# Zero products, row-block results, casts and exponents' arguments placed anew at the start of a retention and feed-forward kernel

## The chip, the cores and the metric

The kernel runs on one core of a Trainium2 chip. A core has TensorE (PE; its weight loads are listed as PEld), VectorE (DVE), ScalarE (ACT), GpSimd (POOL) and SyncE (SP, which here issues the loads). The metric is the device time in microseconds (us), lower is better. Four runs of the kernel before gave 191.04, 191.81, 189.85 and 191.72 us, median 191.38.

## The reference

Four batches, eight heads, 768 positions, head size 64. Each head keeps a 64x64 state that decays by a factor of its own, and the result goes through a multiplicative feed-forward block:

```python
gamma = 1.0 - 2.0 ** (-5.0 - np.arange(H))
for t in range(S):
    state = gamma * state + einsum('bhd,bhe->bhde', k[:, :, t], v[:, :, t])
    y[:, :, t] = scale * einsum('bhd,bhde->bhe', q[:, :, t], state)
x = y.transpose(0, 2, 1, 3).reshape(B * S, H * D)      # 3072 x 512
a = x @ w1                                             # 512 x 1024
b = x @ w2                                             # 512 x 1024
h = a * b @ w3                                         # 1024 x 1024
out = h @ w_out                                        # 1024 x 512
```

## The kernel before

**The whole.** The recurrence is computed by chunks of 128 positions: masked products of queries and keys within a chunk (`scores`, `intra`), plus the effect of the state carried over (`kv`, `state`, `inter`). The decays are folded into scale factors: `VS` on the values, `YS` on the outputs, `GS` on the state. Nothing is multiplied between `w3` and `w_out`, so the kernel first computes their product, `W3O = w3 @ w_out`, in eight row blocks of 128 rows. Then it goes through 12 steps of two batches and one chunk each; a step does attention for one chunk and the feed-forward products of the chunks before. The first two units are special: `Pairs(0)` and `Pairs(1)`, named b0 and b1, are two chunks together of batch 0 and of batch 1.

**Order.** The order is written by hand (`manual_schedule`): each engine executes its instructions as they stand in the program, and each waits for what it reads and for the buffer that it writes.

**The start, in which the change lies.** SP issues all loads in one row (lines 131 to 157): pieces of `w3` and `w_out`, then `q`, `k`, `v` of batch 0, `w1`, the same of batch 1, `w2`, and the later chunks. They land in a ring of 22 stages (`stg`). At most eight loads are under way, since each waits for the one eight places ahead of it.

For row blocks 0 to 5, one block `f` goes in two halves `h`. `cast_w3(f, h)` (line 246) casts half a block to 16 bits: on VectorE for the first halves of blocks 0 to 3, on ScalarE for the others (they show as L239). `w3_half(f, h)` (line 262) transposes it with four TensorE products (L269) and lets VectorE copy the result to `w3t` (L274). `cast_wo(i)` casts two of the eight row groups of `w_out`, half on ScalarE (L243), half on GpSimd (L244). `w3_part(f, i)` (line 293) adds two products of 128x512 (L298) to the accumulator `acc[f]`, a bank of PSUM; with i = 3, the last two, it also lets VectorE copy the bank to `W3O[f]` (L303). Accumulators 0 and 1 lie in banks Y0 and Y1, which the transposes of batch 0's queries and keys take over; 2 to 5 lie in a pool of four banks, from which rows 6 and 7 and then the feed-forward products take theirs.

Row blocks 6 and 7 are done whole: `cast_w3_row` (L255), `w3_transpose` (L280, with a copy to `w3t` on ScalarE, L239), and `W3Block`, whose `mm` adds products (L312) and whose `back` copies the bank to `W3O` on ScalarE (L319).

`busy(m, f)` (line 723) puts m products of zeros, 128x256, into the accumulator of block f before its first real product starts it anew. They compute nothing that is used.

`output_decays()` (line 216) makes `YS`: three products of 128x256 on VectorE (L219, the exponents' arguments `ys_x`), and for each an exponential on ScalarE (L223).

b0 and b1 follow: `q_cast` and `k_cast` (L333), transposes (L371; their copies show as L237 on VectorE), scores (L472) with a mask on VectorE (`am`, L479), `intra` (L493), `kv` (L510), `state` (L521), `inter` (L541), `outputs_back` (L552), and the next state (L526 on VectorE, then L533 on GpSimd). Between their steps stand the first feed-forward products of `w1` and `w2` (`by_rows`, L838), whose four banks include the one of row block 7, and the casts of `w1` (L817) and `w2` (L871, L872, L884). The later steps' products show as L679 and L706.

Of the kernel before, what the change touches and what calls it, by code (L numbers as in the profile page):

```python
# [18 lines left out]
def kernel(  # L19
# [11 lines left out]
    nc = tc.nc  # L31
# [176 lines left out]
    def decays():  # L208
        for h in range(H):
            for s in range(2):  # L210
                nc.gpsimd.memset(LGP[half((h + s) % 2), s, h // 2 : h // 2 + 1], math.log(gam[h]))
        for h in range(H):
            p, r = h // 2, (h % 2) * 64
            nc.gpsimd.memset(GS[r : r + 64, p : p + 1], gam[h] ** C)

    def output_decays():
        for n, (s, swap) in enumerate(((0, 0), (1, 0), (1, 1))):
            x = fsb.tile([128, NP, L], FP, tag="pa", name="ys_x", bufs=8)
            nc.vector.tensor_tensor(  # L219
                x[:, :, :], if_f[:, s, :].unsqueeze(1).broadcast_to((128, NP, L)),  # L220
                LGP[:, swap, :].unsqueeze(2).broadcast_to((128, NP, L)), MULT,
            )
            nc.scalar.activation(YS[:, n, :, :], x[:, :, :], AF.Exp)  # L223
# [7 lines left out]
    W3O = [wpool.tile([128, DM], HP, name=f"w3o_{i}") for i in range(8)]  # L231
# [3 lines left out]
    def cast_to(dst, src, on_dve):  # L235
        if on_dve:
            nc.vector.tensor_copy(dst, src)  # L237
        else:
            nc.scalar.copy(dst, src)  # L239

    def cast_wo(i):
        dst = WO[i][:, :, :].rearrange("p a n -> p (a n)")
        nc.scalar.copy(dst[:, 0:512], wo_st[i][:, 0:512])  # L243
        nc.gpsimd.tensor_copy(dst[:, 512:1024], wo_st[i][:, 512:1024])  # L244

    def cast_w3(f, h):
        W3h[f, h] = att.tile([128, 1024], HP, tag="qT", name="w3h", bufs=5)
        cast_to(W3h[f, h][:, 0:512], w3_st[f][:, h * 512 : h * 512 + 512], h == 0 and f < 4)

    def cast_w3_row(f, *engs):  # L250
        W3h[f] = att.tile([128, 1024], HP, tag="qT", name="w3h", bufs=5)
        n = 1024 // len(engs)
        for i, eng in enumerate(engs):
            cs = slice(i * n, i * n + n)
            (nc.scalar.copy if eng is nc.scalar else eng.tensor_copy)(W3h[f][:, cs], w3_st[f][:, cs])  # L255

    def bank(tag, shape, dtype, name):
        return ps_at.tile(shape, dtype, tag=tag, name=name)
# [3 lines left out]
    def w3_half(f, h):  # L262

        src = W3h.pop((f, h))
        ps = bank(("X0", "X1")[len(units) % 2], [128, 512], HP, "psW3")
        units.append(f)
        for g in range(4):
            c0 = (g // 2) * 256 + g % 2
            nc.tensor.transpose(  # L269
                ps[:, g * 128 : (g + 1) * 128], src[:, c0 : c0 + 255 : 2], ident16[:, :]  # L270
            )
        if h == 0:
            w3t[f] = att.tile([128, 1024], HP, tag="k16" if f < 3 else "v16", name="w3t", bufs=3)
        nc.vector.tensor_copy(w3t[f][:, h * 512 : h * 512 + 512], ps[:, :])  # L274

    def w3_transpose(f, on_dve):
        src, ps = W3h.pop(f), ps_f.tile([128, 1024], HP, tag="psF", name="psW3")
        for g in range(8):
            c0 = (g // 2) * 256 + g % 2
            nc.tensor.transpose(  # L280
                ps[:, g * 128 : (g + 1) * 128], src[:, c0 : c0 + 255 : 2], ident16[:, :]
            )
        w3t[f] = att.tile([128, 1024], HP, tag="k16" if f == 6 else "v16", name="w3t", bufs=3)
        cast_to(w3t[f][:, :], ps[:, :], on_dve)

    acc = {}

    def acc_of(f):
        if f not in acc:
            acc[f] = bank(f"Y{f}", [128, DM], FP, "psW") if f < 2 else ps_f.tile([128, DM], FP, tag="psF", name="psW")  # L290
        return acc[f]

    def w3_part(f, *parts):

        for i in parts:
            for r in range(2):
                g = i * 2 + r
                nc.tensor.matmul(  # L298
                    acc_of(f)[:, :], lhsT=w3t[f][:, g * 128 : (g + 1) * 128], rhs=WO[i][:, r, :],
                    start=(g == 0), stop=(g == 7),  # L300
                )
            if i == 3:
                nc.vector.tensor_copy(W3O[f][:, :], acc[f][:, :])  # L303

    class W3Block:
        def __init__(self, f):
# [8 lines left out]
                )  # L315
            self.g += n

        def back(self):
            nc.scalar.copy(W3O[self.f][:, :], self.ps[:, :])  # L319

    q16s, k16s, v16s, qTs, kTs, AMs, psYs, Ts = {}, {}, {}, {}, {}, {}, {}, {}

    def q_cast(n, *engs):
        if n not in q_in:
            return
        q16s[n] = att.tile([128, 1024], HP, tag="q16", name="q16", bufs=2)
        pairs_cast(q16s[n], q_in.pop(n), *engs)

    def pairs_cast(dst, src, *engs):
        n = H // len(engs)  # L330
        for i, eng in enumerate(engs):
            hs = slice(i * n, i * n + n)
            (nc.scalar.copy if eng is nc.scalar else eng.tensor_copy)(  # L333
                dst[:, :].rearrange("i (t h d) -> i h t d", t=2, d=D)[:, hs, :, :],
                src[:, :].rearrange("i (h t d) -> i h t d", t=2, d=D)[:, hs, :, :],
            )
# [24 lines left out]
    def q_transposes(n, tag, on_dve):  # L361
        qTs[n] = att.tile([128, 2, NP, 128], HP, tag="qT", name="qT", bufs=5)
        pairs_transposes(qTs[n], q16s.pop(n), tag, on_dve)
# [359 lines left out]
    def busy(m, f, n=512):  # L723

        for _ in range(m):
            nc.tensor.matmul(acc_of(f)[:, 0:n], lhsT=Z[:, 0:128], rhs=Z[:, 0:n], start=True, stop=True)
# [2 lines left out]
    busy(12, 0, 256)  # L729
    w3_half(0, 0)  # L730
    cast_wo(0)
    busy(4, 0, 256)
    cast_w3(1, 0)
    w3_part(0, 0)
    w3_half(1, 0)
    busy(1, 1, 256)
    cast_w3(2, 0)
    w3_half(2, 0)
    w3_part(1, 0)
    cast_w3(3, 0)  # L740
    w3_half(3, 0)
    w3_part(2, 0)
    cast_wo(1)
    masks()
    cast_w3(4, 0)
    cast_w3(5, 0)
    cast_w3(0, 1)
    busy(1, 4, 256)
    w3_part(3, 0)
    busy(1, 4, 256)  # L750
    for f in range(4):
        w3_part(f, 1)
    w3_half(4, 0)
    cast_wo(2)
    decays()
    w3_half(5, 0)
# [7 lines left out]
    w3_half(2, 1)  # L764
    w3_part(1, 2)
    cast_wo(3)
    cast_w3(3, 1)
    w3_part(2, 2)
    w3_half(3, 1)
    output_decays()  # L770
    cast_w3(4, 1)
    cast_w3(5, 1)
    for f in range(3):
        w3_part(f, 3)
    q_cast(0, nc.gpsimd)
    w3_part(3, 2, 3)
    q_transposes(0, "Y0", True)
    w3_half(4, 1)
    w3_half(5, 1)
    b0, b1 = Pairs(0), Pairs(1)  # L780
    b0.k_cast(nc.vector)
    w3_part(4, 2, 3)
    w3_part(5, 2)
    b0.k_transposes("Y1", True)
    w3_part(5, 3)
    cast_w3_row(6, nc.scalar, nc.gpsimd)
    am_back = b0.scores(0)
    am_back(0)
# [6 lines left out]
    wb = W3Block(6)  # L795
# [7 lines left out]
    last = ended(b0.intra(1), nc.vector)  # L803
    b0.outputs_back(0)
    wb.mm(2)
    wb.back()
    w3_transpose(7, False)
    b0.inter(last)
    b0.next_state_add()
    b0.outputs_back(1)  # L810
    wb = W3Block(7)
# [7 lines left out]
    cast_w1_halves(0, nc.scalar, nc.gpsimd)  # L819
    cast_w1_halves(1, nc.scalar, nc.gpsimd)  # L820
    wb.mm(6)
    wb.back()
    q_cast(1, nc.scalar, nc.gpsimd)
    b1.k_cast(nc.scalar)
    b1.v_cast(nc.gpsimd, 0)
# [203 lines left out]
```

## Time and profile before

| | |
|---|---|
| median of four runs | 191.38 us |
| the profiled execution | 191.04 us, its span 189.3 us |
| mean granted TensorE clock | 0.989 of full |
| busy: PE, PEld, DVE, ACT, POOL | 175.2, 125.7, 111.6, 71.8, 69.0 us |
| PE busy in 0 to 5, 5 to 10, 20 to 25 us | 3.59, 2.25, 2.91 us |
| PE busy in 50 to 60, 60 to 70 us | 9.90, 10.00 us |
| DVE busy in 20 to 25 us | 4.80 us |
| L303 (results of blocks 0 to 5), DVE | 6 of 679 ns |
| L219 (exponents' arguments), DVE | 3 of 623 ns |
| L223 (exponentials), ACT | 3 of 417 ns |
| L333 (batch 0's keys on DVE; batch 1's on ACT) | 678 ns; 1047 ns |
| L533 (product of 128x256, two inputs), POOL | 2 of 612 ns |

A group's line gives the source line, engine, operation, the tiles out and in, the size and the count. The granted clock is the share of its full clock that TensorE's throttle let through. Idle time of an engine matters only where something on the path to the end waits for that engine. Lengths of instructions that follow each other on an engine overlap a little, so starts lie somewhat closer than lengths.

### The profile page before, as it was taken

The page shows a single profiled execution, that of the slowest core. Times are in us where ns is not written, and L with a number is a line of the kernel's source. Part 1 is how long each engine was busy: PE and PEld are TensorE (multiplying, and loading weights), DVE is VectorE, ACT ScalarE, POOL GpSimd, SP SyncE. Part 2 cuts the span into 40 slices and gives each one's busy share as a digit, 9 for nine tenths or more (in the row PEclk, how much of TensorE's full clock was granted, in tenths as well). Part 3 has the DMA queues.
Part 4 walks back from the last instruction along what each step waited for, and adds up shares of the span by engine and source line. Part 5 has one row for each costly group of instructions (what it writes and reads, how often), then busy time and mean ns, then how long its engine had stood idle before and what let it go on. Part 6 is the DMA issues. An engine that isn't in the chain of part 4 may idle for free.

```text
span 189.3 us, 6242 instructions
## 1 busy us (share of the span) xinstructions
PE 175.2 (93%) x2635; PEld 125.7 (66%) x2635; DVE 111.6 (59%) x214; ACT 71.8 (38%) x158; POOL 69.0 (36%) x125
## 2 busy tenths in 40 slices
PE   7489588968999999999999999999999999999993
PEld 4145354636785769688596785867858688585872
DVE  2424996165165977864847657467495674946330
ACT  3164525712764033243333433424334243332432
POOL 3175252501982294084411836126434260000000
PEclk9999999997999999999999999999999999999999
DMA  5999999999899989979998999989999980110203
GB/s 171 361 401 338 338 372 273 353 382 229 185 274 210 180 276 218 162 201 242 192 217 176 184 240 154 262 175 229 279 172 209 223 167 3 59 55 3 111 0 113
DMA packets 80396, 39.72 MB, mean 210 GB/s; under 512 B 57457, under 2 KB 74097, under 8 KB 80369
## 3 DMA queue, kind: packets, MB, share of 16 engines
q1 hardware_dynamic: 79936, 38.81, 88.7%
q10 hardware_dynamic: 432, 0.52, 0.7%
q8 instruction: 20, 0.33, 0.7%
q14 instruction: 8, 0.06, 0.1%
HBM read 29.36 MB, written 6.29 MB: 188 GB/s over the span
## 4 chain that ended last, share of the span: by engine, by line
PE 72%; DMA 10%; SPq 9%; issue 5%; ACT 1%; POOL 1%; ACTq 0%; POOLq 0%
PE psF L679 39%; PE psO L706 22%; DMA stg<-in_moe_w_dram 10%; SPq L63 9%; PE psY L574 2%; PE psY L642 2%; PE psA L426 2%; PE psF L838 2%; PE psK L594 1%; PE psTk L400 1%; PE psG L679 1%; POOL w L871 1%; ACT w L239 1%; PE psTq L371 0%; ACT osb L710 0%
## 5 line engine op out<-in xcount | busy, mean ns | idle before, releaser
L679 PE MATMUL psF<-xt,w 128*128 128x256 f16 x672 | 76.5, 273 | 0.0
L679 PEld LDWEIGHTS <-w 128*128 128x128 f16 x704 | 68.4, 98 | 11.2 <-issue 0.8
L694 DVE TENSOR_TENSOR ht<-pa,psF 128x256 f16<-128x256 f32 x88 | 36.9, 421 | 37.1 <-PE psF L679 31.4
L706 PE MATMUL psO<-w3o,ht 128*128 128x512 f16 (+2 forms) x200 | 43.9, 371 | 0.0
L688 ACT COPY pa<-psF 128x256 f32<-128x256 f32 x80 | 29.7, 372 | 37.1 <-PE psF L679 37.1
L706 PEld LDWEIGHTS <-ht 128*128 128x128 f16 x200 | 18.5, 98 | 19.4
L710 ACT ACTIVATE osb<-psO 128x512 f32<-128x512 f32 (+2 forms) x25 | 14.5, 580 | 43.5 <-PE psO L706 42.4
L657 DVE TENSOR_TENSOR xt<-psY,YS 64x512 f16<-64x512 f32 (+1 forms) x29 | 21.1, 728 | 4.8 <-PE psY L642 4.4
L353 POOL TENSOR_TENSOR v<-stg,VS 128x512 f16<-128x512 f32 x20 | 20.5, 1043 | 0.8 <-DMA stg<-in_v_dram 0.7
L346 POOL CAST k<-stg 128x512 f16<-128x512 f32 x18 | 10.9, 613 | 21.9 <-DMA stg<-in_k_dram 15.6
L609 POOL TENSOR_TENSOR t<-s,GS 128x512 f16<-128x512 f32 x8 | 8.3, 1040 | 24.5 <-DVE s L608 24.5
L333 POOL CAST q<-stg 128x1024 f16<-128x1024 f32 (+1 forms) x12 | 12.0, 1005 | 12.1 <-DMA stg<-in_q_dram 11.2
L298 PE MATMUL psW<-wo,w3t 128*128 128x512 f16 x48 | 12.5, 380 | 2.7 <-DVE w3t L274 1.7
L433 DVE TENSOR_TENSOR am<-psA,keep 128x512 f16<-128x512 f32 x20 | 12.8, 682 | 0.6 <-PE psA L426 0.6
L838 PE MATMUL psF<-xt,w 128*128 128x256 f16 x64 | 9.8, 297 | 0.2
L274 DVE COPY w3t<-psW 128x512 f16<-128x512 f16 x12 | 4.9, 421 | 7.6 <-PE psW L269 7.6
L298 PEld LDWEIGHTS <-w3t 128*128 128x128 f16 x48 | 4.0, 97 | 6.8 <-DVE w3t L274 3.4
L838 PEld LDWEIGHTS <-w 128*128 128x128 f16 x64 | 6.3, 105 | 2.4 <-ACT w L239 0.4
L616 DVE TENSOR_TENSOR t<-psK,t 128x512 f16<-128x512 f32 x9 | 6.2, 690 | 0.7 <-PE psK L594 0.5
L269 PEld LDWEIGHTS <-w3h 128*128 128x128 f16 x48 | 3.2, 98 | 5.1 <-DVE w3h L237 3.7
L269 PE MATMUL psW<-ident,w3h 128*128 128x128 f16 x48 | 4.5, 220 | 2.1 <-DVE w3h L237 2.0
L458 POOL TENSOR_TENSOR v<-stg,VS 128x512 f16<-128x512 f32 x4 | 4.1, 1042 | 5.1 <-DMA stg<-in_v_dram 2.9
(89 smaller groups left out, 150.4 us busy)
## 6 DMA issues: line engine op xcount, KB each, us to landing
stg<-in_q_dram SPq DMA_DIRECT2D x12, 512.0 KB, 7.1
out_dram<-osb SPq DMA_DIRECT2D x22, 256.0 KB, 3.0
stg<-in_moe_w_dram SPq DMA_DIRECT2D x10, 512.0 KB, 8.6
stg<-in_k_dram SPq DMA_DIRECT2D x20, 256.0 KB, 5.3
stg<-in_v_dram SPq DMA_DIRECT2D x20, 256.0 KB, 6.0
stg<-in_moe_w_dram SPq DMA_DIRECT2D x12, 256.0 KB, 6.9
stg<-in_moe_w_out_dram SPq DMA_DIRECT2D x4, 512.0 KB, 6.9
stg<-in_k_dram SPq DMA_DIRECT2D x2, 512.0 KB, 9.8
```

The costliest lines, as they stand in the source:

```text
L63: nc.sync.dma_start(dst, src)
L298: nc.tensor.matmul(acc_of(f)[:, :], lhsT=w3t[f][:, g * 128 : (g + 1) * 128], rhs=WO[i][:, r, :], start=(g == 0), stop=(g == 7),)
L333: (nc.scalar.copy if eng is nc.scalar else eng.tensor_copy)(dst[:, :].rearrange("i (t h d) -> i h t d", t=2, d=D)[:, hs, :, :], src[:, :]. ...
L353: eng.tensor_tensor(v16[:, e, :].rearrange("j (h d) -> j h d", d=D), v32[:, e, :].rearrange("j (h d) -> j h d", d=D), VS[:, 2, :].unsqueez ...
L433: nc.vector.tensor_tensor(am[:, r, :, :], ps[r][:, :, :], keep[:, :].unsqueeze(1).broadcast_to((128, NP * 2, L)), MULT,)
L657: nc.vector.tensor_tensor(XT[m][to, :, s, :].rearrange("p (a e) (i t) -> p a e t i", e=2, t=2), psYs[m][s][fr, :, :].rearrange("p (a e) (t ...
L679: nc.tensor.matmul(ps[:, :], lhsT=W[d][:, f * 128 : (f + 1) * 128], rhs=self.x(d), start=(d == 0), stop=(d == 3),)
L688: nc.scalar.copy(self.pa[f][:, :], ps[:, :])
L694: nc.vector.tensor_tensor(self.HT[:, f, :], self.pa.pop(f)[:, :], ps[:, :], MULT)
L706: nc.tensor.matmul(psO[:, :], lhsT=self.HT[:, f, e * 128 : (e + 1) * 128], rhs=W3O[f][:, cs], start=(f == 0), stop=(f == 7),)
L710: nc.scalar.activation(osb[:, cs], psO[:, :], AF.Copy, scale=final_scale)
L838: nc.tensor.matmul(ps[f // 2][:, f % 2, :], lhsT=W[d][:, f * 128 : (f + 1) * 128], rhs=f0.x(d), start=(d == 0 and f % 2 == 0), stop=(d == ...
```

## The change

Five things are done to the order of the first 48 us; the amount of real work stays as it is.

1. `output_decays()` makes its three products on GpSimd, and is called one step earlier: ahead of `cast_w3(3, 1)`.
2. The copies of the results of row blocks leave `w3_part` and become calls of their own, `w3_back(f, on_dve)`: blocks 0, 2, 3, 4 on VectorE, 1 and 5 on ScalarE, each at a place of its own.
3. The products of blocks 2 and 3 with the second group of `w_out` move behind the transposes of `(4, 0)`; block 3's last products are split around the transposes of batch 0's queries.
4. Casts: batch 0's keys go from VectorE to ScalarE. With `wb.back(True)`, row block 7's result goes from ScalarE to VectorE, which takes it out of the way of batch 1's queries and keys on ScalarE. Row block 6's result comes behind the copy of the transposes of row 7.
5. Seven more products of zeros: 4 to 6, 1 to 2 at three places, and 2 new ones ahead of `w3_half(3, 0)`.

```diff
@@ output_decays
-            nc.vector.tensor_tensor(
+            nc.gpsimd.tensor_tensor(
                 x[:, :, :], if_f[:, s, :].unsqueeze(1).broadcast_to((128, NP, L)),
...
@@ w3_part
-            if i == 3:
-                nc.vector.tensor_copy(W3O[f][:, :], acc[f][:, :])
+
+    def w3_back(f, on_dve):
+        cast_to(W3O[f][:, :], acc[f][:, :], on_dve)
...
@@ W3Block
-        def back(self):
-            nc.scalar.copy(W3O[self.f][:, :], self.ps[:, :])
+        def back(self, on_dve=False):
+            cast_to(W3O[self.f][:, :], self.ps[:, :], on_dve)
...
     w3_half(0, 0)
     cast_wo(0)
-    busy(4, 0, 256)
+    busy(6, 0, 256)
     cast_w3(1, 0)
     w3_part(0, 0)
     w3_half(1, 0)
-    busy(1, 1, 256)
+    busy(2, 1, 256)
     cast_w3(2, 0)
     w3_half(2, 0)
     w3_part(1, 0)
     cast_w3(3, 0)
+    busy(2, 3, 256)
     w3_half(3, 0)
...
-    busy(1, 4, 256)
+    busy(2, 4, 256)
     w3_part(3, 0)
-    busy(1, 4, 256)
-    for f in range(4):
-        w3_part(f, 1)
+    busy(2, 4, 256)
+    w3_part(0, 1)
+    w3_part(1, 1)
     w3_half(4, 0)
+    w3_part(2, 1)
+    w3_part(3, 1)
...
     cast_wo(3)
+    output_decays()
     cast_w3(3, 1)
     w3_part(2, 2)
     w3_half(3, 1)
-    output_decays()
+    w3_part(0, 3)
+    w3_back(0, True)
+    q_cast(0, nc.gpsimd)
     cast_w3(4, 1)
+    w3_part(1, 3)
+    w3_part(2, 3)
+    w3_part(3, 2)
     cast_w3(5, 1)
-    for f in range(3):
-        w3_part(f, 3)
-    q_cast(0, nc.gpsimd)
-    w3_part(3, 2, 3)
     q_transposes(0, "Y0", True)
     w3_half(4, 1)
+    w3_part(3, 3)
     w3_half(5, 1)
+    w3_back(1, False)
+    w3_back(2, True)
+    w3_back(3, True)
     b0, b1 = Pairs(0), Pairs(1)
-    b0.k_cast(nc.vector)
+    b0.k_cast(nc.scalar)
     w3_part(4, 2, 3)
     w3_part(5, 2)
     b0.k_transposes("Y1", True)
     w3_part(5, 3)
+    w3_back(4, True)
+    w3_back(5, False)
     cast_w3_row(6, nc.scalar, nc.gpsimd)
...
     wb.mm(2)
+    w3_transpose(7, False)
     wb.back()
-    w3_transpose(7, False)
     b0.inter(last)
...
     wb.mm(6)
-    wb.back()
+    wb.back(True)
     q_cast(1, nc.scalar, nc.gpsimd)
     b1.k_cast(nc.scalar)
     b1.v_cast(nc.gpsimd, 0)
```

## The prediction

> **What bounds the kernel now.** I read first the chain of work that ended last, then each engine's timeline up to 50 us, then the granted clock by stretches. Rows of the chain give start, length (us) and work; rows of a timeline start, length, engine, line, operation, tiles, and in brackets the idle time before and what ended it.
>
> ```profile
> PE 72%; DMA 10%; SPq 9%; issue 5%; ACT 1%; POOL 1%; ACTq 0%; POOLq 0%
> ...
> 30.81 6.80 DMA stg<-in_moe_w_dram
> 37.66 0.61 POOL w L817
> 38.27 8.54 issue
> ...
> 47.40 1.05 POOL w L871
> 48.49 1.05 PE psF L838 x8
> ```
>
> From 48.49 us on the chain is almost all TensorE, and the change touches nothing there. So the time moves with the moment at which this dense part begins, and only the first 48 us need working out. Loads fill that stretch (busy share of the DMA engines about 1.0 from 5 to 46 us), yet the last eight of it are "issue": a chain of small steps between PE, VectorE and GpSimd. I follow that chain back.
>
> ```profile
> 18.51 1.71 DVE L219 TENSOR_TENSOR ys_x<-if_f,LGP 128x256 f32<-128x256 f32 x3
> 20.15 2.47 DVE L303 CAST w3o<-psW 128x512 f16<-128x512 f32 x4
> 22.54 0.67 DVE L237 COPY qT<-psTq 128x1024 f16<-128x1024 f16 x1
> ...
> 16.59 0.62 ACT L239 CAST w3h<-stg 128x512 f16<-128x512 f32 x1 [0.22 <-DMA stg<-in_moe_w_dram]
> 19.59 1.09 ACT L223 ACTIVATE YS<-ys_x 128x256 f32<-128x256 f32 x3 [2.38 <-DVE ys_x L219]
> ...
> 27.31 1.01 ACT L239 COPY w3t<-psW 128x1024 f16<-128x1024 f16 x1 [3.86 <-PE psW L280]
> ```
>
> VectorE works without a gap from 18.2 to 24.5 us; TensorE waits for it with batch 0's query transposes (20.88) and twice more. ScalarE idles meanwhile, but its copy of w3t[6] at 27.31 to 28.32 releases row block 6's products (28.44), and from there TensorE runs in program order to 31.95.
>
> ```profile
> 33.10 1.90 PE L312 MATMUL psW<-wo,w3t 128*128 128x512 f16 x8 [0.80 <-ACT w3t L239]
> 34.83 1.65 PE L838 MATMUL psF<-xt,w 128*128 128x256 f16 x12
> 36.32 0.61 PE L371 MATMUL psTq<-ident,q 128*128 128x128 f16 x8
> ...
> 37.21 0.61 PE L371 MATMUL psTq<-ident,k 128*128 128x128 f16 x8
> ...
> 35.03 0.59 ACT L319 CAST w3o<-psW 128x512 f16<-128x512 f32 x1 [0.96 <-PE psW L312]
> 35.52 0.62 ACT L333 CAST q<-stg 128x512 f16<-128x512 f32 x1
> 36.04 1.05 ACT L333 CAST k<-stg 128x1024 f16<-128x1024 f32 x1
> ```
>
> Here TensorE is nearly without a gap from block 7 (33.10) to batch 1's key transposes (37.21). The casts of q and k end at 36.14 and 37.09, both only just in time.
>
> ```profile
> 38.26:41.67 3.41, 2.10 (x53) 1.40 (x54) 2.77 (x5) 0.38 (x1) 0.01 (x1) 1.00 1.03 396
> 41.67:45.08 3.41, 3.41 (x64) 2.36 (x60) 1.06 (x2) 0.79 (x2) 0.00 (x0) 0.50 1.18 291
> ```
>
> The columns are PE, PEld, DVE, ACT, POOL, clock, DMA share, GB/s. After a stretch of small products TensorE ran 3.41 us at half clock, on the path.
>
> **What the Trainium skill says.** "TensorE: Matmul & The Clock Gate", Part 1: the array's clock is halved after a window of about 3.4 us without enough activity, and the windows run freely, so where they fall differs between executions. The 3.41 us at 0.50 agree; that the runs (189.85 to 191.81) differ for this reason is my inference. The same page, under "Architectural detail", says that ScalarE, VectorE and GpSimd work strictly in order; the trace shows no overtaking, and my main term rests on it. "GPSIMD Engine Reference", section 3.1, prices a GpSimd product of two tensors at about 2.6 cycles an element: an estimate from it is 256 x 2.6 / 1.2 GHz = 0.55 us plus dispatch for 128x256. The nearest row, L533 (128x256, also two inputs), took 0.61; I use that.
>
> **The change part by part.**
>
> *Exponents' arguments (L219) to GpSimd, exponentials ahead of the cast of W3 half (3,1).* VectorE loses 1.71 us. GpSimd gets three products behind its cast of wo[3], which ends at 16.76 (16.15 + 0.61). Starts come about 0.57 apart, so they end near 17.35, 17.9 and 18.5; its q cast, before at 18.24, starts near 18.5. On ScalarE the three L223 now stand ahead of the cast of half (3,1), whose data was there at 16.59. The third waits for 18.5, ends at 18.9, and the cast runs 18.9 to 19.5 instead of 16.59 to 17.2. Queued behind it are the casts of (4,1) and (5,1), which still end at 20.6 against 21.7 before. TensorE, in order, stops at half (3,1) from about 17.9 to 19.55.
>
> *Results of the row blocks.* L303 issued six VectorE copies at once behind the fourth product pair; now each `w3_back` stands where its bank is needed: 0, 2, 3, 4 on VectorE, 1 and 5 on ScalarE, and batch 0's key cast (0.68 on VectorE) goes to ScalarE (1.05, as L333 of batch 1). From 19.55: transposes of (3,1) 0.22, eight products of 0.216 (1.73), so batch 0's query transposes start at 21.5 (before 20.88). W3O[0] is out by 21.05, so they no longer wait for VectorE. Then (4,1), two products, (5,1); qT copy 22.1 to 22.8, the w3t copies to 23.5, six products 23.15 to 24.45, key transposes at 24.45 (before 24.91), kT copy 25.1 to 25.8 (before 25.56 to 26.25), scores 25.85 (before 26.30). VectorE's relief comes to 0.45 us.
>
> *What is late next.* On ScalarE `w3_back(5)` waits for block 5's last product (about 25.5) and runs to 26.15; behind it is the cast of W3 row 6, which ran at 22.84 before, now 26.1 to 26.7. The transposes of row 6 wait for it: 26.75 (before 26.66), w3t[6] out at 28.4 (before 28.32). So row block 6 starts at 28.45 against 28.44: the 0.45 us ends in this wait. With its errors: -0.3 to +0.4 us.
>
> *Block 7 and batch 1's casts.* w3t[7]'s copy moves ahead of W3O[6]'s on ScalarE. Before, W3O[6] ended at 32.13 and the transposes at 31.95: 0 to 0.05 gained. W3O[7] goes to VectorE (about 0.68, as L303, against 0.59). Its bank is the fourth of `by_rows`, so TensorE's seventh L838 waits for it: +0.1. With W3O[7] gone, the q and k casts start about 0.85 us earlier (near 34.65 and 35.2 instead of 35.52 and 36.04; q landed at 30.9, k at 32.6). But TensorE's order ahead of the key transposes is full: gain at most 0.1, lost again to the bank.
>
> *Zeros.* Seven more products of 128x256, about 0.11 each at full clock. Two stand in the wait for wo[0] (to 5.80), one in that for w3h (8.42), two before half (3,0) (9.68), one before w3t (10.54): hidden. The last delays the products at 11.15 by 0.11, which the wait of 0.30 at 13.78 takes in, also made shorter by half (4,0) standing two blocks earlier. Cost 0. If a window falls badly, they may prevent half clock near 8 to 12 us: 0 to -0.5.
>
> *Queues.* SP's loads keep order and buffers; its waits there are for earlier loads and for casts long done, so no transfer moves. The q cast of batch 0 on GpSimd goes 0.2 later, past nothing that waits (the next is a load at 22.8).
>
> Sum: 0 - 0.05 + 0.1, about +0.1. The profiled execution took 191.04 (span 189.3 and 1.7 around it), giving 191.14; it lies 0.34 under the median, so I forecast 191.5.
>
> **The rivals.**
> *Clock.* In the low stretch TensorE's groups took 1.03 for four products (0.61 elsewhere), 0.64 for 16 of L493 (0.42), 0.64 for 32 of L510 (0.45) and 1.75 for eight (1.05): 1.5 us more. If zeros and order shift the work so that it keeps full clock in most runs: 191.5 - 1.5 = 190.0. For: the spread of the runs is of this size. Against: the batch 1 stage keeps its small products and waits.
> *The earlier casts count in full.* 0.85 off: 190.6. Against: TensorE is full from 33.10 to 37.21.
> *The other side: the stall at half (3,1).* The chain after it has no slack left, so what GpSimd takes longer is paid one for one. At 1.04 a product (the row of 128x512) the third ends at 19.8: +1.3, or 192.8; a stall of 3 us may then also halve the clock for work on the path, up to +1.7, or 194.5. It decides over 1% once the third product ends after about 20.3. For: nothing else may run on ScalarE meanwhile. Against: L533's 0.61.
> *A change that does nothing* is my forecast by another road: the new order is there on each engine, but waits trade places.
>
> **How the numbers follow.** Trade 0.54 (191.5, own range 190.9 to 192.2), clock 0.19 (190.0), early casts 0.08 (190.6), stall 0.19 (192.8). This kernel's measurement tells about 1% from no change, 1.9 us: faster means under 189.5, reached only if the clock gain adds to a better chain, 0.15; slower means over 193.3, the stall with its clock loss, 0.17; within 0.68. Range 189.7 to 193.1.
>
> **What would show it.** L219 on POOL three times at 0.6; a TensorE gap near 17.9 to 19.5; the query transposes of batch 0 no longer waiting for DVE w3o; ScalarE's cast of row 6 near 26; row block 6 near 28.5; block 7 near 33.1; batch 1's key transposes within 0.3 us of 37.2. Wrong if w3t[6] is out well before 28, or if the dense part starts over 1 us away from 48.5 at the same clock.

## The result and the profile after

The changed kernel took 192.03 us (median of 36 runs, 189.87 to 194.87) beside 191.04 us (57 runs) of the kernel before on the same chip. The ratio is 1.0044, with a 95% interval of 1.0022 to 1.0067: slower by 0.84 us, 0.42 to 1.28. The forecast was 191.5, that is +0.1 against the runs before it. A ratio counts only the runs within 1.5% of the fastest of its kernel, which drops many runs at a low granted clock, while a median is one of all runs.

The profiled execution took 192.01 us and spans 189.9. Its timeline up to row block 7 (start, length, engine, line, operation, tiles, and in brackets the idle time before it and what ended it):

```profile
16.23 1.75 POOL L219 TENSOR_TENSOR ys_x<-if_f,LGP 128x256 f32<-128x256 f32 x3
...
18.02 0.42 ACT L223 ACTIVATE YS<-ys_x 128x256 f32<-128x256 f32 x1 [0.15 <-POOL ys_x L219]
18.34 1.64 ACT L239 CAST w3h<-stg 128x512 f16<-128x512 f32 x3
...
19.00 0.40 PE L269 MATMUL psW<-ident,w3h 128*128 128x128 f16 x4 [1.43 <-ACT w3h L239]
...
20.96 0.61 PE L372 MATMUL psTq<-ident,q 128*128 128x128 f16 x8
...
25.14 0.59 ACT L239 CAST w3o<-psW 128x512 f16<-128x512 f32 x1 [2.62 <-PE psW L298]
25.63 0.62 ACT L255 CAST w3h<-stg 128x512 f16<-128x512 f32 x1
...
26.30 0.62 PE L280 MATMUL psW<-ident,w3h 128*128 128x128 f16 x8 [0.42 <-ACT w3h L255]
26.96 1.01 ACT L239 COPY w3t<-psW 128x1024 f16<-128x1024 f16 x1 [0.71 <-PE psW L280]
...
28.03 0.61 PE L313 MATMUL psW<-wo,w3t 128*128 128x512 f16 x2 [0.29 <-ACT w3t L239]
...
32.64 1.90 PE L313 MATMUL psW<-wo,w3t 128*128 128x512 f16 x8 [0.76 <-ACT w3t L239]
...
34.58 0.69 DVE L237 CAST w3o<-psW 128x512 f16<-128x512 f32 x1 [1.93 <-PE psW L313]
```

The reader sees the predicted chain. GpSimd makes the three arguments, ScalarE's third exponential ends at 18.4, and only then comes the cast of half (3,1), for which TensorE stands still 1.43 us. Later ScalarE's copy of W3O[5] (25.14) keeps the cast of row 6 until 25.63, and TensorE waits 0.42 for it. All starts lie about 0.45 us ahead of the predicted ones, because loads landed 0.45 us earlier in this execution (W3's half (1,1) at 13.30 instead of 13.77, the cast of batch 1's v began at 34.00 instead of 34.48). The same piece landed anywhere from 13.04 to 14.37 in the profiles of this document, and at 13.04 when the changed kernel ran again, so this is taken as chance of one execution and not as the change.

The stretches by engine, in the columns that the prediction explains:

```profile
37.96:41.38 3.42, 2.16 (x53) 1.46 (x54) 2.72 (x5) 0.00 (x0) 0.00 (x0) 1.00 1.05 369
41.38:44.79 3.41, 3.41 (x60) 2.28 (x59) 1.07 (x2) 0.91 (x2) 0.00 (x0) 0.50 1.21 278
```

The window at half clock lies where it lay before (41.67 to 45.08), so the two executions can be compared. The chain of waits of after (start, length, work):

```profile
48.14 1.05 PE psF L850 x8
...
64.49 1.19 PE psO L707 x5
65.68 0.55 issue
66.22 2.54 PE psO L707 x11
...
136.68 0.36 PE psK L595 x31
137.04 0.05 issue
137.09 0.20 ACT mark L631
137.29 0.04 issue
```

The dense part starts at 48.14 against 48.49, and after adding the 0.45 of the loads that is +0.1, as forecast. But from there to the end of the span it is 141.76 us against 140.8: **0.95 us are lost where the change touches nothing**. The larger part is a stop of TensorE at 65.68 that waits for nothing in the profile: two products start 0.92 us apart there, where 0.21 is usual, so 0.71 are lost (the chain's 0.55 counts from the modelled end of the product ahead). In the kernel before the same 16 products run through, as its timeline shows; and ScalarE's small copy "mark", which orders two groups of TensorE's products, is released by psY:

```profile
64.77 3.63 PE L706 MATMUL psO<-w3o,ht 128*128 128x512 f16 x16
...
136.42 0.19 ACT L630 COPY mark<-zeros 1x1 f16<-1x1 f16 x1 [0.52 <-PE psY L574]
```

After, in the same view, it is released one group of products later, and is part of the chain:

```profile
137.09 0.19 ACT L631 COPY mark<-zeros 1x1 f16<-1x1 f16 x1 [0.81 <-PE psK L595]
```

From psK's start to the next group L642 (L643 after) it is 0.58 us before (136.13 to 136.71) and 0.82 after (136.51 to 137.33): 0.24 us. With the 0.71 that is the whole 0.95 of this pair of executions.

### The profile page after: what moved, and what is told of

Same layout as the page of the kernel before. It is cut to its first block, busy times and chain, and to the rows that moved or that the text cites. A ratio compares the mean times of both kernels' runs of the same rounds, so it can differ in the third digit from the quotient of the medians.

```text
span 189.9 us, 6257 instructions
## 1 busy us (share of the span) xinstructions
PE 177.1 (93%) x2642; PEld 126.7 (67%) x2642; DVE 109.1 (57%) x209; ACT 73.5 (39%) x160; POOL 70.5 (37%) x128
## 4 chain that ended last, share of the span: by engine, by line
PE 71%; DMA 12%; issue 6%; SPq 6%; POOL 2%; ACT 1%; ACTq 0%; POOLq 0%
PE psF L680 39%; PE psO L707 22%; DMA stg<-in_moe_w_dram 6%; DMA stg<-in_v_dram 6%; SPq L63 6%; PE psY L575 2%; PE psY L643 2%; PE psF L850 2%; PE psA L427 1%; PE psK L595 1%; POOL v L459 1%; PE psTk L401 1%; PE psG L680 1%; POOL w L883 1%; ACT w L239 1%
## 5 line engine op out<-in xcount | busy, mean ns | idle before, releaser
L354 POOL TENSOR_TENSOR v<-stg,VS 128x512 f16<-128x512 f32 x20 | 20.5, 1042 | 2.2 <-DMA stg<-in_v_dram 2.2
L298 PE MATMUL psW<-wo,w3t 128*128 128x512 f16 x48 | 13.3, 389 | 0.4 <-DVE w3t L274 0.3
L727 PE MATMUL psW<-zeros 128*128 128x256 f16 x26 | 5.8, 374 | 1.3 <-DVE zeros L160 1.3
```

The source lines that it names most:

```text
L298: nc.tensor.matmul(acc_of(f)[:, :], lhsT=w3t[f][:, g * 128 : (g + 1) * 128], rhs=WO[i][:, r, :], start=(g == 0), stop=(g == 7),)
L354: eng.tensor_tensor(v16[:, e, :].rearrange("j (h d) -> j h d", d=D), v32[:, e, :].rearrange("j (h d) -> j h d", d=D), VS[:, 2, :].unsqueez ...
```

## The experiments

Three theories. **A**: waits trade places ahead of 48 us, as forecast, and the rest is chance. **B**: the change makes the windows at half clock more frequent or puts them on the path. **C**: the added zeros move all later instructions of TensorE by 14 places in its stream (seven products, seven weight loads), and something in the supply of that stream stops TensorE. Each group of four ran on one chip with its own runs of the kernel before.

### Group 1: the zeros and the exponents' arguments

*ctl_before*: the kernel before, unchanged.

> The kernel before, unchanged, timed as a kernel of its own so that each of its runs has a granted clock beside its time. Theory A (waits trade places ahead of 48 us; the rest is chance): ratio 1.000, and among runs without a low-clock window (clock 1.00) it is 0.1 to 0.3 us faster than the changed kernel's 190.3. Theory B (the change makes low-clock windows more frequent): the runs at clock 1.00 agree within 0.1 us with the changed kernel's, but they are a larger share than the changed kernel's 7 of 36. Theory C (TensorE's instruction stream stalls in the dense part of the changed kernel): at equal clock this one is 0.5 us or more faster.

Measured: ratio 0.999, 0.9954 to 1.0027, so no bias is seen beyond 0.5 points. Its three runs at a recorded clock of 1.00 took 191.40 to 191.96 us, over 1 us more than the changed kernel's 190.3. None of the theories had expected that: recorded clock does not make runs equal, as the last section shows.

*no_zeros*: the change without its seven further zeros.

```diff
-    busy(6, 0, 256)
+    busy(4, 0, 256)
...
-    busy(2, 3, 256)
...
```

> The changed kernel with the seven added products of zeros taken out again. Theory A: same time as the changed kernel at equal clock, within 0.2 us. Theory B: the share of runs at clock 1.00 moves away from 7 of 36. Theory C (seven more weight loads and products shift TensorE's instruction stream): the gap of 0.55 us in the products of L707 near 65.7 us goes, and the time returns to that of before.

Measured: 1.0042, 1.0001 to 1.0084. Taking the zeros out of the change gives nothing that can be told from the change. Theory C had expected the time of the kernel before: a miss. Its profile has no stop near 65 us, but the late mark (0.80 behind psK), and it stands still 1.11 us at half (3,1).

*ys_later*: the change with `output_decays()` back behind the transposes of half (3,1), still on GpSimd.

```diff
-    output_decays()
     cast_w3(3, 1)
     w3_part(2, 2)
     w3_half(3, 1)
+    output_decays()
```

> The changed kernel with the exponents' arguments still on GpSimd, but the call back behind the transposes of W3 half (3,1), so that ScalarE's cast of that half is not queued behind three exponentials. Theory A: TensorE's gap of 1.43 us ahead of the transposes of (3,1) goes, and the chain behind it, which has no slack until loads bind it, comes 1 to 3 us earlier: ratio to before 0.985 to 0.995. Theories B and C: nothing moves by more than 0.3 us at equal clock, ratio 1.00 to 1.01.

Measured: **0.9931**, 0.99 to 0.9962, within what theory A expected and faster than both kernels. The stop at half (3,1) is gone from its profile:

```profile
19.18 0.39 PE L269 MATMUL psW<-ident,w3h 128*128 128x128 f16 x4
```

Near 64.3 us TensorE stops as it does in after, and loses 1.05 us.

*ys_only*: the kernel before with the arguments on GpSimd and the call ahead of `cast_w3(3, 1)`.

> The kernel before with only the first part of the change: the exponents' arguments on GpSimd, and their call ahead of the cast of W3 half (3,1). Theory A: the gap ahead of the transposes of (3,1) appears as in the changed kernel, VectorE no longer has 1.71 us of products but still six result copies and the key cast; the dense part begins 0.3 to 0.5 us later than before, ratio 1.001 to 1.004. Theories B and C: as before, ratio 1.000.

Measured: 0.9955, 0.9925 to 0.9985. A miss for all three: this part alone is faster, neither slower nor neutral. In its profile TensorE ran at half rate up to 13.9 us, reached half (3,1) only at 20.31, and did not wait there. Why it is faster stays open: the profiled execution took 0.73 us less than that of ctl_before, which was at half rate as long, and 0.63 of that is a stop of ctl_before that the next group treats.

### Group 2: the stream of TensorE

Counting TensorE's records in the profiles (5,270 in each kernel without the further zeros) gave theory C a shape. The stop of after (65.68) and that of ys_later (64.32) both stand ahead of its instruction number 1473, and ctl_before had one at 125.51 (0.63 us lost), ahead of number 3521. Both numbers are 193 plus a multiple of 256. The page of after has a queue for this supply (packets, MB, share of 16 engines):

```profile
q8 instruction: 20, 0.33, 0.7%
```

20 packets of 16 KB come for about 5,300 instructions, about one for 256. In the trace the packet ahead of the stop starts at 63.78 (after), 62.60 (ys_later) and 123.34 (ctl_before), and TensorE goes on 2.44, 2.60 and 2.61 us after that start. Where TensorE did not stop, at these places and at all others of this kind, 2.7 us or more lay between such a place and its packet. Shifted by 14 places, number 1473 falls among slow products ahead of 66 us, about 1.5 us sooner than without.

*zeros_late*: the kernel before with seven narrow zeros in TensorE's wait near 45.7 us, so that only the places move.

```diff
     b1.inter()
+    pz = bank("X1", [128, DM], FP, "psZ")
+    for _ in range(7):
+        nc.tensor.matmul(pz[:, 0:64], lhsT=Z[:, 0:128], rhs=Z[:, 0:64], start=True, stop=True)
     b1.outputs_back(1)
```

> The kernel before, with seven products of zeros of 64 columns put into TensorE's wait for xt near 45.7 us (0.8 us idle there in the kernel before), so that all later instructions of TensorE stand 14 places (7 products, 7 weight loads) further on in its stream and nothing before that wait is changed. Theory C, the stream: in the profiles so far every unexplained stop of TensorE in the dense part stands ahead of an instruction whose number is 193 plus a multiple of 256 (1473 in the kernel after, 3521 in the kernel before run again), one 16 KB packet of the instruction queue comes for every 256 instructions, and the stop ends 2.4 to 2.6 us after that packet's start. With the shift, number 1473 lies 1.5 us earlier in the dense work, so the profile shows a stop of 0.3 to 0.9 us ahead of it near 65.5 us, and the ratio is 1.002 to 1.005. Theory B (the zeros only move the clock's windows) and theory A (only waits of the first 48 us): no stop there, ratio 0.999 to 1.001.

Measured: 1.0011, 0.9979 to 1.0042. Its 16 products took 3.83 us instead of 3.63: 0.2 us lost at number 1473.

```profile
64.12 3.83 PE L706 MATMUL psO<-w3o,ht 128*128 128x512 f16 x16
```

The place is right, the size at the lower end, and the ratio tells nothing from no change.

*after_wide*: the change with seven zeros of 512 columns in place of fourteen of 256.

```diff
-    busy(6, 0, 256)
+    busy(3, 0, 512)
...
-    busy(2, 1, 256)
+    busy(1, 1, 512)
...
```

> The kernel after with its fourteen short zeros of 256 columns made into seven of 512, so that their time on the array stays and TensorE's stream has the places of the kernel before. Theory C: the stop of 0.55 us near 65.7 us is gone, and with it most of what the change cost: ratio to the kernel before 0.999 to 1.002 (the kernel after: 1.0044). Theory B: the clock's windows stay as in the kernel after, and so does the ratio, 1.003 to 1.006. Theory A: the rest of the change's loss lies in the new order ahead of 48 us, ratio 1.003 to 1.006.

Measured: 1.0009, 0.9979 to 1.0038; no stop near 65 us, the mark late as in after. This is where theory C put it, but it is not shown: the interval reaches nearly to after's ratio, and the median of all runs is 191.69 us beside 190.80, which is as much as the change lost.

*ys_later_wide*: both edits.

> As after_wide, and the three products of the exponents' arguments with their exponentials back behind the transposes of half (3,1). Theory C: 0.5 us under the same without wide zeros (0.9931), so 0.989 to 0.992. Theories A and B: no change against it, 0.992 to 0.995.

Measured: 0.996, 0.9931 to 0.9989. A miss for all three theories, which had set it against 0.9931 on another chip. Beside after_wide, which shares its chip, it is 0.5 points lower, and its products show what the stop at half (3,1) holds up:

```profile
17.27 0.39 PE L269 MATMUL psW<-ident,w3h 128*128 128x128 f16 x4
17.50 1.89 PE L298 MATMUL psW<-wo,w3t 128*128 128x512 f16 x8
19.22 0.61 PE L372 MATMUL psTq<-ident,q 128*128 128x128 f16 x8
...
26.47 0.60 PE L313 MATMUL psW<-wo,w3t 128*128 128x512 f16 x2 [0.29 <-ACT w3t L239]
```

With loads as early as in after (the piece named above at 13.37), batch 0's query transposes come 1.74 us ahead of after's (20.96), and row block 6 is still 1.56 us ahead (28.03). The wait for row 6 is no fixed point in time, as ScalarE's copy of W3O[5] moves with TensorE.

*row6_first*: ys_later_wide with the cast of row 6 ahead of the copy of W3O[5].

```diff
     w3_back(4, True)
-    w3_back(5, False)
     cast_w3_row(6, nc.scalar, nc.gpsimd)
+    w3_back(5, False)
```

> As ys_later_wide, with ScalarE's cast of W3 row 6 ahead of its copy of W3O[5]. Theory A (row 6's transposes wait for ScalarE's copy of W3O[5], 0.43 us in the kernel after): that wait goes, row block 6 starts 0.3 to 0.4 us earlier, and if the loads of W3 row 7 and of batch 1 don't take it back, the ratio is 0.2 points under ys_later_wide's: 0.987 to 0.990. The rival: the next wait (the w3t copy of row 7, the loads of batch 1) is late by as much, and the ratio stays ys_later_wide's within 0.001.

Measured: **0.9899**, 0.9867 to 0.9931, the best version and faster than both kernels. The range is theory A's, but the step from ys_later_wide is 0.6 points where theory A expected 0.2, and the wait that goes accounts for no more than that; the rest is not explained. The profiled execution is one of its slowest (192.74 us, its granted clock at half from 8.15 to 14.97 and from 42.28 to 45.69), so its starts can't be set beside those above, and only the order of waits is read from it. Row 6's transposes follow the scores without a wait for ScalarE; a wait of 0.30 for VectorE comes next:

```profile
27.06 0.42 PE L473 MATMUL psA<-qT,kT 64*64 64x128 f16 x16 [0.35 <-DVE kT L237]
27.41 0.62 PE L280 MATMUL psW<-ident,w3h 128*128 128x128 f16 x8
28.33 0.41 PE L473 MATMUL psA<-qT,kT 64*64 64x128 f16 x8 [0.30 <-DVE am L480]
```

### Group 3: the parts alone, and the change again

*zeros_only*: the kernel before with the further zeros.

```diff
-    busy(4, 0, 256)
+    busy(6, 0, 256)
...
+    busy(2, 3, 256)
     w3_half(3, 0)
...
```

> The kernel before with the seven further zeros alone. Theory C (the zeros shift TensorE's stream by 14 places, so that its instruction 1473 stands 1.5 us sooner behind the start of the packet it needs): a stop of 0.2 to 0.9 us ahead of 1473 near 65.5 us, ratio 1.001 to 1.005. Theory B (the zeros change where the clock's low windows fall): low windows ahead of 15 us become shorter or rarer than in the kernel before, and the ratio may lie on either side, 0.995 to 1.005, without such a stop. Theory A: 0.999 to 1.001.

Measured: **0.9952**, 0.9915 to 0.999. Theory C expected a loss: a miss. Theory B allowed a gain. At number 1473 it lost only 0.1 us, and the zeros brought more than that. It ran at full rate from 4.8 us to the end in its profile. The next section shows what that is worth.

*rows_only*: the kernel before with the new order of row blocks and results, without the rest.

```diff
-            if i == 3:
-                nc.vector.tensor_copy(W3O[f][:, :], acc[f][:, :])
+    def w3_back(f, on_dve):
+        cast_to(W3O[f][:, :], acc[f][:, :], on_dve)
...
```

> The kernel before with the new order of the row blocks' products and results alone (batch 0's key cast on ScalarE with it). By the steps of the prediction without the stop at half (3,1): the query transposes of batch 0 no longer wait for VectorE's copies of W3O, and what is gained ends in the wait of row 6's transposes for ScalarE: ratio 0.996 to 1.000. In every kernel with the whole new order the mark of ScalarE near 136 us waits for the products of psK instead of psY and TensorE starts the output products 0.2 us later; if this order is what brings it, it is here and not in b1_only.

Measured: 0.9961, 0.9931 to 0.9991, a ratio as expected. But its median over all runs is 191.09 us beside 190.86, so that this part is faster at all is not shown. And in its profile the query transposes still waited 0.39 us for VectorE's copy of W3O, which was to go. The mark is released by psY (0.52), so this part alone does not make it late.

*b1_only*: the kernel before with batch 1's casts and W3O[7] in the new places.

```diff
     wb.mm(6)
-    wb.back()
+    wb.back(True)
...
```

> The kernel before with w3t[7]'s copy ahead of W3O[6]'s and W3O[7]'s on VectorE alone, so that ScalarE's casts of batch 1's queries and keys start sooner. The prediction's term: -0.05 for block 7, +0.1 for the bank that VectorE's copy gives back later: ratio 0.9995 to 1.001. The rival (the earlier casts count in full): 0.996. If the late mark near 136 us comes from this part, 0.2 us more.

Measured: 1.0003, 0.9971 to 1.0036. This agrees with the prediction's term, and the rival's 0.996 lies outside. The mark is released by psY here too.

*after_again*: the change, unchanged.

> The kernel after, unchanged, beside its parts. Theory C: its profile again shows the stop ahead of TensorE's instruction 1473 (0.2 to 0.9 us), the mark 0.2 us late, and the ratio is 1.002 to 1.007. If the first profile's stop was chance, it is absent here.

Measured: 1.004, 1.0009 to 1.0072; the mark late again (0.81 behind psK), the stop at half (3,1) again (1.44 us). No stop at number 1473 this time: the profile missed what theory C expected, though the ratio lies in its range. So that stop comes in some executions. The five profiles with the shift lost 0.71, 1.05, 0.2, 0.1 and 0 us at number 1473, 0.41 in the mean, and none at 3521. None of the nine without it lost anything at 1473; three of them did at 3521 (0.63, 0.28 and 0.11; 0.11 in the mean of nine). The places move with the stream: that much is shown. That TensorE waits for the packet is inferred from the times alone. By these means, an estimate from few and widely scattered values, the shift costs 0.3 us.

## Why the prediction held, and what it missed

*Exponents' arguments.* Right in mechanism and size: 0.6 us a product on GpSimd (1.75 for three), the third exponential at its end, the stop at half (3,1) (1.43 us, forecast 1.65), the query transposes near 21.5 (20.96 with loads 0.45 earlier). "GPSIMD Engine Reference", section 3.1 of the Trainium skill, gave 0.55 us plus dispatch as an estimate; the trace agrees with 0.61. The profile of ys_only also says why the call did no harm there: TensorE came late to half (3,1).

*Results of the row blocks, and what is late next.* Right: the cast of row 6 behind W3O[5], the wait of 0.42, row block 6 at 28.48 on the old loads' time (predicted 28.45). The text let the gain of 0.45 us end in row 6's wait. The runs show a better reading: without the stop at half (3,1) the whole chain, row 6 included, comes 1.6 us earlier. What could be gained upstream was eaten by the stop first. Row 6's wait costs something too, since row6_first is faster than ys_later_wide.

*Why three gains alone make no gain together.* Zeros, arguments and row order alone give 0.9952, 0.9955 and 0.9961, the last of them a doubtful gain. In the change TensorE waits at half (3,1) for ScalarE's queue, whose end is set by GpSimd's cast of wo[3] and three products, whatever TensorE did sooner; what the zeros bring ahead of it ends there. This account is argued, not tested part by part. It fits no_zeros (taking them out of the change costs nothing), ys_later, and the pair after_wide and ys_later_wide. By these two pairs the stop costs 0.5 to 1.1 points, 0.9 to 2.1 us (in the first the zeros differ too, and the two intervals of the second overlap a little).

*Block 7 and batch 1's casts.* Right: batch 1's key transposes at 36.86 with loads 0.45 earlier (37.31; before 37.21), W3O[7] on VectorE in 0.69, and b1_only at 1.0003, which can't resolve terms of 0.1 us.

*Zeros, "cost 0".* This term was **mis-sized**, on both sides. On the gain's side, my profile of before was warm (at full rate) from 4.05 us, so nothing was to be gained in it. ctl_before shows the other case. Its timeline has half rate at 11 us,

```profile
11.21 1.06 PE L298 MATMUL psW<-wo,w3t 128*128 128x512 f16 x2
```

where zeros_only has full rate at the same work:

```profile
10.02 0.59 PE L298 MATMUL psW<-wo,w3t 128*128 128x512 f16 x2
```

In zeros_only six of ten runs, those with a recorded clock of 1.0, lie at 189.41 to 189.88, where the 15 such runs of the kernel before on that chip have a median of 191.20. The other four, at 0.991, lie at 191.33 to 192.40. So the term's own "0 to -0.5" came true larger, 0.9 us by the ratio (0.2 to 1.6), and in some executions only. The time is that of the prediction's clock rival (190.0), but the place is another: the start, not the stretch after 41 us. That the zeros keep the start warm is argued from these profiles; ys_later, with the same zeros, had half clock from 8.87 to 12.28 us. On the loss's side, seven products are also 14 places in TensorE's stream, which the sum left out: 0 to 1.05 us at number 1473, some 0.3 net in the mean of the profiles.

*"From 48.49 us on ... the change touches nothing there."* This sentence was wrong. Besides the stream, the mark near 137 us is released by psK, and the next group comes 0.14 to 0.25 us later, in all seven profiles that hold the row order, the arguments on GpSimd and batch 1's casts together, and in none of the seven others. None of the three alone brings it; whether two do was not tried, and what links them to the mark stays open.

*The sum.* +0.1 up to 48 us, +0.3 for the stream, +0.24 for the mark: 0.64 us, where 0.84 (0.42 to 1.28) was measured. The remaining 0.2 is inside the interval. But this sum describes profiles, and the runs do not show one loss in all of them. At a recorded clock of 0.991 the change is slower (21 runs with a median of 192.01; after_again's 12 have 192.18, where before's 29 on its chip have 190.48). At 1.0 it is faster (seven runs with 190.31, where before's on three other chips have 190.94 to 191.56). Both profiles of the change have a half-clock window near 41 to 45 us, on the path. Of the 14 profiles of this document seven have it and seven do not, before among the first and ctl_before among the second. And after_again had a second window, which no profile of before shows:

```profile
28.16:31.57 3.41, 3.41 (x70) 1.60 (x68) 0.27 (x2) 0.51 (x1) 1.23 (x2) 0.50 1.16 291
```

How often such a window lies on the path I could not settle. Theory B may so hold a large share of the loss, and the split between B and C is not shown.

*The forecast's number.* The forecast difference of +0.1 lies outside the measured 0.42 to 1.28. The time fell into the stated range (189.7 to 193.1) because that range was wide enough for terms that the sum did not have: that part is luck. What held is the path up to 48 us.

*The rivals.* The stop was real but ended near the time forecast, so the loss over 1% did not come; the early casts did not count; "does nothing" was near, but by a sum of opposite terms.

## What to carry to other kernels

Before moving work ahead in an engine's queue, find the one instruction behind it that another engine needs, and ask what sets that moment: a stop there can swallow what is gained upstream, so parts that each help can lose together. A part should be judged in the whole as well as alone, and in more than one execution, since one profile may have had the clock that hides its worth. "It touches nothing there" holds for the program's order, not for the places of instructions in an engine's stream nor for where a signal is given.

## What the runs showed of the hardware

- A recorded clock of 1.0 does not mean full rate from the start. In ctl_before the record begins with full clock at 13.5 us, the profile's stretches give 1.00 ahead of it, and yet two products of 128x512 took 1.06 there (11.21, above) and 0.59 later:

```profile
14.72 0.59 PE L298 MATMUL psW<-wo,w3t 128*128 128x512 f16 x2
```

  "TensorE: Matmul & The Clock Gate", Part 1, of the Trainium skill has half rate as the default until a busy window has passed; the durations agree, the recorded mean hides it.
- TensorE's instructions came in packets of 16 KB, about one for 256 (20 for about 5,300). The seven stops of 0.1 us and more that the groups above count stood ahead of number 1473 or 3521, both 193 plus a multiple of 256, and ended 2.4 to 2.8 us after the start of the packet before. A few places more or fewer in the stream move these points to other work.
